# Turning 46 weight blocks early, one by one, through a 1 KB tile into DRAM, and loading them plainly for the last pass

## The chip, the cores and the metric

One core of a Trainium2 chip runs the kernel. The metric is the device time of one execution in microseconds (us). The engines are TensorE (PE; PEld for its weight loads), VectorE (DVE), ScalarE (ACT), GpSimd (POOL) and SyncE (SP), each with its own in-order stream of instructions. All five share 16 DMA engines. Transfers are issued from queues: SyncE's is q1 in the profile, POOL's is q0, ScalarE's is q10.

## The reference

The kernel computes the output of a small network and all gradients of it (12 tensors), for 2048 positions of 576 channels, in bf16.

```python
def _B_ref(x, w1, w3, w2):
    gate = jnp.einsum("bsd,df->bsf", x, w1)
    up = jnp.einsum("bsd,df->bsf", x, w3)
    h = _silu(gate) * up
    return jnp.einsum("bsf,fd->bsd", h, w2)

x = A_u
xn = _layernorm(x, axis=-1)
s = _A_ref(xn, ...)              # a long convolution over the positions, made from A, B, C, log_dt
g = _silu(_B_ref(xn, B_w1, B_w3, B_w2))
out = x + s * g
# returned: out, and the vjp of all of it at grad_out for A_u, the convolution's
# parameters and w1, w3, w2
```

Here w1 and w3 are 576 x 4608 and w2 is 4608 x 576.

## The kernel before

The forward pass (gate and up products, the convolution's kernel, the convolution, the output) takes the first 660 us or so. The function `backward` does the rest.

**Gradient groups.** The 4608 hidden columns are cut into 18 groups of 256 (`NG = 18`). For group `gi`, `phase6_group` makes the gradient at the hidden layer in four steps (stages `h0` to `h3`, matmuls of L1818), which VectorE multiplies onto the tiles `gu_n` and `gg_n` (L1836). These are stored to `GU_dram` and `GG_dram` on SyncE (L1841, stage `stored`). `phase6_grad13` then makes the gradients of w3 and w1 (stages `out_11_0` to `out_11_3`, `out_10_0` to `out_10_3`, matmuls of L1882). `phase6_grad2` makes those of w2 (L1859), one half after `h1`, one after `h3`. ScalarE copies each product out of PSUM (two buffers, `pgw`) into `gw` tiles, and POOL stores them (`grad_store`, L1867).

**What feeds a group.** POOL loads `gg_n` (L1759) and `h_n` (L1744), 1 MB each, two groups ahead into pairs of buffers. ScalarE and VectorE prepare the next group's `gg_n`, `gu_n` and `h_n` from `h3` of the group before on (`phase6_prep`: silu at L1786, its derivative at L1789, products at L1782 and L1783). SyncE turns the block of w2 of a group (`w2T`, L1739) out of rows that it loaded (`w2r`, L1718).

**Beside the groups.** During groups 0 to 5 the backward convolution (`ssm_bwd_conv`) runs on the same engines. Its loads `a` and `gs` and its stores to `gK_dram` go through SyncE. From the end of group 10 on `param_step` reduces the convolution's parameter gradients on VectorE (L1453, L1456), fed by `qT`, `gz` and `pz` through SyncE.

**The last pass.** `phase6_inputs` makes the gradient at the normalized input: for each of 16 blocks of 128 positions, 72 steps of matmuls (L1931) over the 36 column blocks of w1 and of w3. The left operand, `acts`, is `GG_dram` and `GU_dram` turned by SyncE. The right operand is w1 and w3 turned, as blocks of 128 columns by 576: 26 blocks in `wA`, which groups 12 to 16 load, and 46 blocks in eight pieces `wT`. A piece takes the place of a tile that the groups no longer need (`h_n`, `gg_n`, `gu_n`, `w2T`), so it can come only at the end: `load_piece` issues it between group 16 and the beginning of the last pass, with a transfer that turns.

**Order.** Instructions are placed by a scheduler that follows priorities and due times (`at`). `issue_after` puts an instruction behind another in that order. `sp`, `gp` and `sc` chain the instructions of SyncE, POOL and ScalarE in the order in which the code issues them (`sp` only from group 10 on).

The names and lines in the profile are those of this listing:

Of the kernel before, what the change touches and what calls it, by code (L numbers as in the profile page):

```python
# [14 lines left out]
BF16 = mybir.dt.bfloat16  # L15
I32 = mybir.dt.int32
I16 = mybir.dt.int16
P = 128
# [82 lines left out]
class K:  # L101
# [25 lines left out]
    def pool(self, **kw):  # L127
        return self.tc.tile_pool(reuse_waits="tile", **kw)
# [1440 lines left out]
    def backward(self, T0, TG, TQ, TC, TX, gctx, mats):  # L1569
        nc, cfg = self.nc, self.cfg  # L1570
        D, L, LT, F, FT = cfg.D, cfg.L, cfg.LT, cfg.F, cfg.FT
# [6 lines left out]
        pool = self.pool  # L1578
        PS = bass.MemoryType.PSUM
        GP, FE = 11, FT - self.FG // P  # L1580
        with ExitStack() as out:
# [7 lines left out]
            ffn = ExitStack()  # L1589
            elp = out.enter_context(pool(name="e_el", bufs=3))  # L1590
            self.small = out.enter_context(pool(name="e_sm", bufs=1))
            gwp = ffn.enter_context(pool(name="e_gw", bufs=2))
            self.at(T0 - TG)
            self.w2rows = [rowp.tile([P, self.FG // P, cfg.DT * P], BF16, name=f"w2r{i}") for i in range(2)]
            for w2r in self.w2rows:
# [50 lines left out]
            for gi in range(NG):  # L1646
# [9 lines left out]
                for stage in group if gi == 0 else self.phase6_group(gi, cur, elp, gwp, ps_h, ps_gw):  # L1656
                    if stage == "h3" and self.chain and gi + 2 < NG:
                        self.w2Ts[gi + 2] = self.phase6_load_w2(gi + 2, wp)
                    if stage == "h3" or stage[:-1] in ("out_11_", "out_10_") and stage != "out_10_3":
                        next(prep, None)  # L1660
                    if stage in ("h1", "h3"):
                        if gi < NG - 1:
                            w2(gi, stage == "h3")
                        if stage == "h3" and gi + 2 < NG:
                            self.phase6_load_h(gi + 2, T0 + TG * gi, inp)
# [47 lines left out]
    def w2row_load(self, gi):  # L1713
        D = self.cfg.D
        nfl = self.FG // P
        for fl in range(nfl):
            fi = gi * nfl + fl
            self.sp(lambda: self.nc.sync.dma_start(out=self.w2rows[gi % 2][:, fl, 0:D],  # L1718
                                                   in_=self.aps["B_w2"][fi * P:(fi + 1) * P, :]))

    def load_piece(self, wT, pool, tag, ai, f0, n):
        t = pool.tile([P, n, self.cfg.D], BF16, name=f"wT{ai}_{f0}", tag=tag)
        wT.append((ai, f0, n, t))
        self.nat_transpose(t[:], self.aps[("B_w1", "B_w3")[ai]][:, f0 * P:(f0 + n) * P])

    def load_wT_rows(self, part, c):
        ai, f0, n, t = part
# [384 lines left out]
```

## Time and profile before

| | |
|---|---|
| Median of 3 runs | 1701.79 us (1697.92 to 1708.54) |
| The profiled execution's own time | 1704.94 us |
| Its span in the profile | 1703.2 us |
| Mean granted TensorE clock | 0.988 |
| TensorE busy | 1601.0 us, 94% |
| VectorE busy | 1396.6 us, 82% |
| ScalarE busy | 852.8 us, 50% |
| POOL busy | 488.3 us, 29% |
| Time of q1's packets (SyncE) | 64.2% of 16 engines |
| Time of q0's packets (POOL) | 20.5% of 16 engines |
| Time of q10's packets (ScalarE) | 4.0% of 16 engines |

The span runs from the first to the last instruction of the program on the core; the execution's own time holds a little more. Busy time of an engine leaves out the instructions that only issue transfers, wait or branch. All of SyncE is of that kind, so it has no busy time: it is seen through its transfers. A line such as `A L1 <- B L2: 4.6, 3, 1.7` says that A at line 1 waited for B at line 2 for 4.6 us in all, three times, for 1.7 us at most. For a transfer, two durations stand apart: how long its issue held the engine, and "to landing", from the start of the issue until the data had arrived. The landing is known for only some of them.

### The profile page before, as it was taken

The page shows a single profiled execution, that of the slowest core. Times are in us where ns is not written, and L with a number is a line of the kernel's source. Part 1 is how long each engine was busy: PE and PEld are TensorE (multiplying, and loading weights), DVE is VectorE, ACT ScalarE, POOL GpSimd, SP SyncE. Part 2 cuts the span into 40 slices and gives each one's busy share as a digit, 9 for nine tenths or more (in the row PEclk, how much of TensorE's full clock was granted, in tenths as well). Part 3 has the DMA queues.
Part 4 walks back from the last instruction along what each step waited for, and adds up shares of the span by engine and source line. Part 5 has one row for each costly group of instructions (what it writes and reads, how often), then busy time and mean ns, then how long its engine had stood idle before and what let it go on. Part 6 is the DMA issues. An engine that isn't in the chain of part 4 may idle for free. (4 is left out here: it accounts for less than half of the span.)

```text
span 1703.2 us, 34846 instructions
## 1 busy us (share of the span) xinstructions
PE 1601.0 (94%) x13615; PEld 1178.2 (69%) x13615; DVE 1396.6 (82%) x2114; ACT 852.8 (50%) x1536; POOL 488.3 (29%) x786
## 2 busy tenths in 40 slices
PE   6799999999998999999999999999999988999998
PEld 2455555544445777788788788888888866877876
DVE  8779999897974555998996999699999946879765
ACT  6689999866652113756556565555555301000001
POOL 6746676533242111111111111111111252031132
PEclk9899999999999999999999999999999999999999
DMA  7789999989899889766585757799999999999992
GB/s 236 279 307 367 348 366 325 356 284 293 261 274 229 207 197 191 229 197 207 175 218 163 212 181 210 191 259 251 254 217 252 243 243 236 210 200 232 239 205 51
DMA packets 620812, 408.61 MB, mean 240 GB/s; under 512 B 424263, under 2 KB 562007, under 8 KB 616039
## 3 DMA queue, kind: packets, MB, share of 16 engines
q1 hardware_dynamic: 563868, 272.95, 64.2%
q0 software_dynamic: 33984, 114.33, 20.5%
q10 hardware_dynamic: 22794, 19.10, 4.0%
q8 instruction: 107, 1.75, 0.4%
q14 instruction: 59, 0.48, 0.1%
HBM read 128.52 MB, written 189.06 MB: 186 GB/s over the span
## 5 line engine op out<-in xcount | busy, mean ns | idle before, releaser
L1931 PEld LDWEIGHTS <-acts 128*128 128x128 bf16 x2304 | 227.2, 99 | 68.0 <-issue 5.3
L1882 PEld LDWEIGHTS <-xn_bf 128*128 128x128 bf16 x2304 | 224.3, 98 | 35.6 <-issue 9.5
L1453 DVE TENSOR_TENSOR pr_q<-et_ps,pz 128x1024 f32<-128x1024 f32 x144 | 176.1, 1223 | 35.9 <-PE et_ps L1448 27.7
L1867 POOL DMA_DIRECT2D out_dram<-gw x72 | 47.4, 658 | 551.6 <-ACT gw L1884 340.3
L1931 PE MATMUL px<-wT,acts 128*128 128x288 bf16 x1472 | 193.7, 290 | 4.6 <-DMA wT<-in_B_w_dram 4.6
L1456 DVE TENSOR_REDUCE S_all<-pr_q 128x32 f32<-128x1024 f32 x144 | 175.4, 1218 | 3.2
L1074 PEld LDWEIGHTS <-xnT 128*128 128x128 bf16 x1152 | 108.1, 98 | 99.7 <-issue 15.0
L1818 PE MATMUL ph<-w2T,goT 128*128 128x256 bf16 x1440 | 169.1, 273 | 2.3 <-ACT gh L1821 2.3
L1074 PE MATMUL pg<-wmB_w,xnT 128*128 128x512 bf16 x576 | 156.4, 380 | 1.8 <-DVE g_t L1093 1.6
L1074 PE MATMUL pu<-wmB_w,xnT 128*128 128x512 bf16 x576 | 156.8, 379 | 0.0
L1859 PE MATMUL pgw<-go_o,h_n 128*128 128x288 bf16 x1152 | 152.8, 286 | 0.2 <-DVE h_n L1783 0.2
L1818 PEld LDWEIGHTS <-goT 128*128 128x128 bf16 x1440 | 139.2, 98 | 18.8 <-issue 3.0
L1882 PE MATMUL pgw<-gu_n,xn_bf 128*128 128x256 bf16 x1152 | 133.8, 272 | 4.5 <-ACT gw L1863 3.9
L1859 PEld LDWEIGHTS <-h_n 128*128 128x128 bf16 x1152 | 111.8, 98 | 27.6 <-issue 0.8
L1882 PE MATMUL pgw<-gg_n,xn_bf 128*128 128x256 bf16 x1152 | 130.3, 273 | 0.0
L1089 ACT ACTIVATE s_t<-pg 128x512 bf16<-128x512 f32 x144 | 87.4, 607 | 70.5 <-PE pu L1083 51.4
L1821 ACT CAST gh<-ph 128x512 bf16<-128x512 f32 x144 | 80.6, 587 | 79.2 <-PE ph L1818 70.7
L1931 PE MATMUL px<-wA,acts 128*128 128x288 bf16 x832 | 111.7, 291 | 3.5 <-DMA acts<-GU_dram 3.5
L772 POOL COPY KT<-k_s 64x128 bf16<-64x128 bf16 x144 | 95.2, 661 | 66.3 <-ACT k_s L769 61.7
L727 ACT ACTIVATE cs_k<-et_ps 128x512 bf16<-128x512 int16 x216 | 110.3, 627 | 1.1 <-PE et_ps L725 1.0
L1987 ACT ACTIVATE go<-gx 128x576 bf16<-128x576 f32 x16 | 10.9, 683 | 197.8 <-DVE gx L1970 184.2
L1094 ACT CAST u_t<-pu 128x512 bf16<-128x512 f32 x144 | 86.8, 603 | 10.7 <-PE pu L1074 10.5
(308 smaller groups left out, 3120.1 us busy)
## 6 DMA issues: line engine op xcount, KB each, us to landing
U_dram<-u_t POOLq DMA_DIRECT2D x72, 256.0 KB, 4.9
H_dram<-h_t SPq DMA_DIRECT2D x72, 256.0 KB, 5.1
G_dram<-g_t POOLq DMA_DIRECT2D x72, 256.0 KB, 5.1
Q_dram<-q_k SPq DMA_DIRECT2D x36, 512.0 KB, 6.0
gg_n<-G_dram POOLq DMA_DIRECT2D x18, 1024.0 KB, 6.4
h_n<-U_dram POOLq DMA_DIRECT2D x18, 1024.0 KB, 8.1
GG_dram<-gg_n SPq DMA_DIRECT2D x36, 512.0 KB, 7.7
GU_dram<-gu_n SPq DMA_DIRECT2D x36, 512.0 KB, 5.4
```

Source lines behind the costliest of these rows:

```text
L727: self.sin_last = nc.scalar.activation(out=CS[:, :, o:o + 256], in_=pt[:].bitcast(I16)[:, :, 0::2], func=ACT.Sin, scale=6.283184 / 2 ** 16)
L772: nc.gpsimd.tensor_copy(out=KT[64 * hf:64 * hf + 64, :, ch // 9, h, d1:d1 + 8], in_=ks[64 * h:64 * h + 64, :, h, hf].rearrange("p d a -> p ...
L1074: ins = nc.tensor.matmul(pt[:], lhsT=xnT[:, c, ts], rhs=wm[w][:, c, :], start=(q == 0 and c == 0), stop=(q == 1 and c == nfull - 1))
L1089: nc.scalar.activation(out=s_t[:, :, q, :], in_=pgv, func=ACT.Silu)
L1094: self.gate_last = nc.scalar.copy(out=u_t[:, :, q, :], in_=puv)
L1453: nc.vector.tensor_tensor(out=pr[:].rearrange("p r k e -> p r (k e)"), in0=T[x][:].rearrange("p z k h j a -> p (z k h j a)")[:, None].to_b ...
L1456: nc.vector.tensor_reduce(out=self.S_all[:].rearrange("p r (h c) -> p r h c", h=2)[:, :, :, d0:d0 + 2], in_=pr[:].rearrange("p r k (h j a) ...
L1818: self.pe_last = nc.tensor.matmul(ph[j][:, k, :].rearrange("p (a f) -> p a f", f=P), lhsT=lw, rhs=rh, start=(n == 0), stop=(n == nfull))
L1821: self.sc(lambda: nc.scalar.copy(out=gh[:, j], in_=ph[j][:]))
L1859: self.pe_last = nc.tensor.matmul(pgw[pi_][:, 0:pw], lhsT=hn[:, tt, fl * P:(fl + 1) * P], rhs=go_o[:, tt, po:po + pw], start=(tt == 0), st ...
L1882: self.pe_last = nc.tensor.matmul(pw_[:, 0:FG], lhsT=self.xn_bf[:, tt, c * P:(c + 1) * P], rhs=nat[:, tt, :], start=(tt == 0), stop=(tt == ...
L1931: self.pe_last = nc.tensor.matmul(px[pi_][:, 0:pw], lhsT=acts[i][:, ai, fi, :], rhs=w[:, po:po + pw], start=(n == 0), stop=(n == len(steps ...
```

## The change

A tile `w_turn` of 128 x 512 (1 KB in each partition, one buffer) is added. At the stages `h0`, `h2`, `out_11_0`, `out_11_2` and `out_10_0` of groups 0 to 10 one step of the generator `turn_weights` is taken: SyncE turns one block of 512 x 128 of w1 or w3 into the tile, and POOL stores the tile into a DRAM scratch `WT`, laid out as the piece will be read. After the blocks of a piece one more step turns what is left of the 576 rows, 64 of them, for all its blocks at once, so eight pieces make 46 + 8 = 54 steps. `load_piece` then loads a piece plainly from `WT`, at the same place in SyncE's order where it turned it before.

```diff
             gwp = ffn.enter_context(pool(name="e_gw", bufs=2))
+            self.turnp = ffn.enter_context(pool(name="e_turn", bufs=1))
+            self.WT = {}
+            turning = self.turn_weights()
...
+                    if gi < GP and stage in self.TURNS:
+                        next(turning, None)
...
+    PIECES = ((1, 22, 7), (0, 15, 7), (1, 15, 7), (1, 13, 2), (0, 22, 7), (0, 29, 7), (1, 11, 2), (1, 29, 7))
+    TURNS = ("h0", "h2", "out_11_0", "out_11_2", "out_10_0")
+
+    def turn_weights(self):
+        nc, D = self.nc, self.cfg.D
+        nfull = D // P * P
+        store = None
+        for ai, f0, n in self.PIECES:
+            w = self.aps[("B_w1", "B_w3")[ai]]
+            dst = self.WT[ai, f0] = self.dram.tile([P, n, D], BF16, name=f"WT{ai}_{f0}")
+            for f in range(n + 1):
+                t = self.turnp.tile([P, nfull], BF16, name="w_turn")
+                if f < n:
+                    src, out, o = w[0:nfull, (f0 + f) * P:(f0 + f + 1) * P], dst[:, f, 0:nfull], t[:]
+                    i = t[:]
+                else:
+                    rem = D - nfull
+                    o = i = t[:, 0:n * rem].rearrange("p (f d) -> p f d", f=n)
+                    src, out = w[nfull:D, f0 * P:(f0 + n) * P], dst[:, :, nfull:D]
+                with self.tc.issue_after(self.pe_last.ins):
+                    self.nat_transpose(o, src)
+                self.gp(lambda: nc.gpsimd.dma_start(out=out, in_=i))
+                yield
+
     def load_piece(self, wT, pool, tag, ai, f0, n):
         t = pool.tile([P, n, self.cfg.D], BF16, name=f"wT{ai}_{f0}", tag=tag)
         wT.append((ai, f0, n, t))
-        self.nat_transpose(t[:], self.aps[("B_w1", "B_w3")[ai]][:, f0 * P:(f0 + n) * P])
+        self.sp(lambda: self.nc.sync.dma_start(out=t[:], in_=self.WT[ai, f0][:]))
```

## The prediction

> **What bounds the kernel now.** I read the page first, then the stretches, then who waits for whom on each engine, then single tiles.
>
> ```profile
> span 1703.2 us, 34846 instructions
> ...
> PE 1601.0 (94%) x13615; PEld 1178.2 (69%) x13615; DVE 1396.6 (82%) x2114; ACT 852.8 (50%) x1536; POOL 488.3 (29%) x786
> ...
> q1 hardware_dynamic: 563868, 272.95, 64.2%
> ```
>
> TensorE is busy for 94% of the span, so only its gaps can be won; q1, the queue of SyncE with all the turning transfers, is the busiest of the queues. The stretches tell the groups from the last pass (columns: stretch, its length, busy time with count of each engine, granted clock, DMA share, GB/s):
>
> ```profile
> core 0: us, PE busy (x) PEld busy (x) DVE busy (x) ACT busy (x) POOL busy (x), PEclk, DMA share, GB/s
> 690.00:1077.00 387.00, 368.58 (x3648) 317.36 (x3646) 353.81 (x635) 226.46 (x409) 46.86 (x79) 1.00 0.68 198
> 1313.00:1400.00 87.00, 78.25 (x711) 64.65 (x709) 67.31 (x99) 23.14 (x44) 29.15 (x54) 0.96 1.13 241
> 1360.00:1400.00 40.00, 33.66 (x276) 26.42 (x275) 21.40 (x47) 3.14 (x8) 18.47 (x35) 0.91 1.16 243
> 1400.00:1450.00 50.00, 43.29 (x364) 34.17 (x363) 31.18 (x36) 4.93 (x9) 13.74 (x25) 0.97 1.10 241
> ```
>
> Gradient groups 0 to 10 lie in the first: TensorE 95% busy, DMA engines at 0.68, which is room. Around the start of the last pass the DMA engines are full (1.10 to 1.16), TensorE stands still for 6.3 and 6.7 us, and its granted clock dips to 0.91 and 0.97. After it there is nothing to win for a while:
>
> ```profile
> 1450.00:1500.00 50.00, 50.00 (x443) 40.65 (x441) 45.27 (x52) 4.13 (x8) 6.88 (x13) 1.00 1.13 191
> ```
>
> TensorE's waits from 1250 us on (who, for whom, us in total, times, longest):
>
> ```profile
> PE px L1931 <- DMA wT<-in_B_w_dram: 4.6, 3, 1.7
> PE et_ps L1448 <- DVE S_all L1456: 4.1, 1, 4.1
> PE px L1931 <- DMA acts<-GU_dram: 3.5, 1, 3.5
> ```
>
> So 4.6 us are the very pieces that the change reloads, 3.5 us the activations queued behind such pieces on SyncE, 4.1 us are VectorE's. In the groups (640 to 1110 us) no DMA is among TensorE's waits; the largest is
>
> ```profile
> PE et_ps L899 <- DVE ZZ L1385: 8.0, 7, 2.5
> ```
>
> **What the change removes.** Eight turning transfers (the wT pieces, 46 blocks of 576x128) leave the end; eight plain loads of the same 6.8 MB take their places in SyncE's order.
>
> ```profile
> L1739 SPq DMA_TRANSPOSE wT<-in_B_w_dram x8: 1350/4170/9025, 1313.4 to 1393.0; - x8
> ```
>
> A piece held SyncE for 4.2 us in the median. The nearest plain load of that size, beside a turned one (name, KB where told, median us to landing):
>
> ```profile
> gg_n<-G_dram POOLq DMA_DIRECT2D x18, 1024.0 KB, 6.4
> ...
> acts<-GG_dram SPq DMA_TRANSPOSE x17, 8.7
> ```
>
> Both are about 1 MB (a full acts half is 36 blocks of 128x128, 1.18 MB), as is a piece of seven blocks (1.03 MB). 8.7 - 6.4 = 2.3 us less for each of 46 / 7 = 6.6 such pieces is 15 us of DMA time gone from a stretch that is full. That is more than the 4.6 + 3.5 = 8.1 us for which TensorE waited on it, so I take both waits as gone. The clock adds (1 - 0.91) x 40 + (1 - 0.97) x 50 = 5.1 us lost at most to dips after those stops; I take half, 2.5. VectorE's 4.1 us stays. Gain: 8.1 + 2.5 = 10.6 us; its ends are 0 (the queue is as full as before, since qT and acts still turn) and 8.1 + 5.1 = 13.2.
>
> The Trainium skill, Advanced Engine Details and Errata, section X-Bar Transpose (TRN2), says that turning transfers are as fast as plain ones. By it the end would gain nothing; 8.7 against 6.4 us here speaks against it, though the rows differ in queue and hour.
>
> **What it adds.** 54 turns (46 blocks of 512x128, 8 remainders), five a group, on SyncE; 54 stores of up to 128 KB on POOL. There is one tile, so turn k+1 waits for the landing of store k, and store k for the landing of turn k: a single chain of round trips. The ordering hint behind TensorE's last matmul only places a turn in SyncE's order; in the built program a turn waits for the store before it, and for no matmul after the first. But both queues run in order, so the chain is tied to what stands between. On POOL a store stands before nearly every gradient store, and the load of the group after next (gg_n) stands behind store five. On SyncE the stores of GU and GG, the loads of w2T and those of the backward convolution (a, gs) stand behind turns.
>
> A turn by its nearest row, the w2T turns of 128x640 in 690 to 1100 us, and a store by that of gw (144 to 256 KB), same stretch:
>
> ```profile
> L1739 SPq DMA_TRANSPOSE w2T<-w2r x22: 1200/1269/5689, 692.2 to 1099.5; - x22
> ...
> DMA to landing us min/median/max: 2.6/2.6/2.6
> ```
>
> ```profile
> L1867 POOL DMA_DIRECT2D out_dram<-gw x42: 545/568/767, 699.4 to 1099.9; - x42
> ...
> DMA to landing us min/median/max: 2.0/4.0/8.2
> ```
>
> One trip is 2.6 + 4.0 = 6.6 us; five are 33.0. Two of the five queue behind something large. One turn follows the GU and GG stores (2 MB) on q1; what a small transfer there pays is the longest of w2r, which stands behind the same stores:
>
> ```profile
> L1718 SPq DMA_DIRECT2D w2r<-in_B_w_dram x18: 328/454/1382, 697.5 to 1073.0; - x18
> ...
> DMA to landing us min/median/max: 2.1/2.6/8.0
> ```
>
> 8.0 - 2.6 = 5.4 us more. One store follows the 1 MB h_n load on POOL's queue:
>
> ```profile
> L1744 POOL DMA_DIRECT2D h_n<-U_dram x10: 538/539/539, 705.9 to 1063.2; - x10
> ...
> DMA to landing us min/median/max: 5.7/9.4/9.8
> ```
>
> issued 0.5 us after it, it lands no earlier: 9.4 - 0.5 - 4.0 = 4.9 us more. A group's chain: 33.0 + 5.4 + 4.9 = 43.3 us. What a group has comes from the first and last gg_n load, ten groups apart:
>
> ```profile
> L1759 POOL DMA_DIRECT2D gg_n<-G_dram x11: 552/552/554, 691.2 to 1077.0; - x11
> ...
> DMA to landing us min/median/max: 5.0/6.8/11.7
> ```
>
> (1077.0 - 691.2) / 10 = 38.6 us. The chain is 4.7 us a group too long, 47 us over ten groups. What is late next: POOL's gg_n load, then ScalarE's first silu of the next preparation, then (ScalarE runs in order) the copies of pgw, whose two buffers stop TensorE. The cover is read from one group:
>
> ```profile
> 781.17 0.54 POOL L1744 DMA_DIRECT2D h_n<-U_dram  x1
> 786.48 0.76 POOL L1867 DMA_DIRECT2D out_dram<-gw  x1 [4.78 <-ACT gw L1884]
> 793.47 0.76 POOL L1867 DMA_DIRECT2D out_dram<-gw  x1 [6.22 <-ACT gw L1884]
> 794.93 0.55 POOL L1759 DMA_DIRECT2D gg_n<-G_dram  x1 [0.70 <-PE pgw L1893]
> ```
>
> ```profile
> 817.15 1.06 ACT L1786 ACTIVATE gu_n<-gg_n 128x1024 bf16<-128x1024 bf16 x1
> ```
>
> 817.2 - 794.9 - 6.8 = 15.4 us, available once and not per group: a lag that stays is paid no more, one that grows is. Cost in the groups: 47 - 15.4 = 31.6 us. The same rows show where it bites: between h_n and gg_n lie 13.8 us, into which three of the five trips fall.
>
> Ends of this cost. Below: trips at the shortest rows, 2.6 + 2.0 = 4.6 us, five are 23.0, with the two delays 33.3, under 38.6: nothing. A gain here has no source, since nothing is taken out of the groups. Above: the turns of the forward pass with other transfers about,
>
> ```profile
> L1739 SPq DMA_TRANSPOSE hcB<-H_dram x10: 1322/1916/5826, 468.1 to 625.6; - x10
> ...
> DMA to landing us min/median/max: 4.4/6.0/8.9
> ```
>
> at their shortest 4.4, make a trip 8.4 and a group's chain 52.3: (52.3 - 38.6) x 10 - 15.4 = 122 us. Some hcB turns are six times as large, so w2T is nearer; and a stretched group thins the other transfers out and shortens its own trips. I take 6.6.
>
> The remainders' stores write 64 elements a run, in 896 runs; no row shows such a store from POOL. I count them as the others; six large ones at twice the median would add 6 x 4.0 = 24 us to the chain, which the upper end holds. The new load lines, the 54 issues on POOL (0.57 us each of an engine that is 12% busy there) and the 54 on SyncE (1.3 us each, 6 us a group) are hidden as such. In the built order part of the convolution's matmuls and products of groups 4 and 5 change places with the groups' own; their counts are the same, and I count nothing; what it costs if they meet late loads is rival B.
>
> **Sum.** 31.6 - 10.6 = +21.0 us on the span of 1703.2, or on its execution's own 1704.94: 1725.9. That execution is 3.15 above the median of the runs, 1701.79, against which I forecast 1701.8 + 21.0 = 1722.8, say 1723, +1.2%.
>
> **The rivals.** A: the chain fits. It decides at (38.6 - 5.4 - 4.9) / 5 = 5.7 us a trip: below it every turn is hidden in the 32% of DMA time that the groups leave free, the end keeps its gain, and the time is 1701.8 - 10.6 = 1691. For it: the share of 0.68, and gw's shortest landing of 2.0, which a store alone on its queue would have. Against it: the median of 4.0 is that of stores which the chain resembles, and the chain adds traffic. The Trainium skill, DMA: Bandwidth & Descriptors, section Anatomy of one DMA, gives about 2 us as the fixed part of a transfer. An estimate from it, 4 us a trip and 20 a group, is this rival; the median of 4.0 for one store of gw says that here the fixed part is not the whole.
>
> B: the chain is far too long, and the convolution's loads (a, gs), late behind it on SyncE, stop VectorE and through it TensorE's in-order matmuls. At 7.6 us a trip: 48.3 a group, 97 - 15.4 - 10.6 = +71 us, 1773. For it: 8.0 and 9.4 us in the rows above; against it, the self-limit.
>
> C: the groups cost what I say and the end gains nothing, because the stretch stays full of qT and acts: 1701.8 + 31.6 = 1733. For it: share 1.13 after 1450 us, where no piece is turned any more.
>
> **How the numbers follow.** The forecast 0.41, A 0.33, B 0.16, C 0.10. The range 1689 to 1773 holds A's 1691 with its full clock gain of 13.2 and B's 1773; what lies beyond is half of B and little of A. The likeliest case alone, trips of 6.2 to 7.0 us, runs from 1703 to 1743. About 1% (17 us) is what a measurement of this kernel can tell from no change. Faster by more than that needs more than the whole of A's gain, 13.2 us: 0.04, taken from A. Within 1%: the rest of A (0.29), the lower third of the forecast (0.14) and 0.01 of C: 0.44. Slower: 0.27 of the forecast, B, and 0.09 of C: 0.52.
>
> **What would show it.** In the changed profile the gg_n loads of groups 0 to 10 stand 42 to 43 us apart instead of 38.6, POOL waits for turns landing (w_turn) ahead of its stores, SyncE for stores (WT) landing ahead of turns, and TensorE's busy share there falls from 95% to about 88%. At the end TensorE's waits for wT and acts are gone and the clock stays near 1. Wrong I am if gg_n loads keep their 38.6 us (A), if they stand over 46 us apart or VectorE waits for a or gs (B), or if TensorE still waits for weights or activations at 1360 to 1405 us plus the shift (C).

## The result, and the profile after

The changed kernel takes 1770.24 us in the median of 6 runs, the kernel before 1704.22 us on the same chip: a ratio of 1.0388 (95% interval 1.0343 to 1.0434), 66 us slower. The forecast was 21 us slower; 1770 lies just inside its range, 1689 to 1773. The profiled execution took 1774.58 us. Lines after the new function lie 29 lower than before: L1788 is the gg_n load (before L1759), L1773 the h_n load, L1768 every turning transfer, L1815 the first silu, L1811 and L1812 VectorE's products, L1847 and L1850 the hidden layer's matmuls and ScalarE's copies of them, L1870 the stores of GU and GG, L1892 ScalarE's copy of a w2 product, L1911 the matmuls of the w1 and w3 gradients, L1896 the gradient stores, L1960 the last pass. L1747 is the new store, L1753 the new plain load.

The page of the changed kernel:

```profile
span 1772.8 us, 34974 instructions
...
PE 1611.2 (91%) x13555; PEld 1186.9 (67%) x13615; DVE 1399.7 (79%) x2114; ACT 852.7 (48%) x1536; POOL 517.5 (29%) x840
...
q1 hardware_dynamic: 566492, 279.74, 65.1%
```

TensorE's work is the same, and its share is down from 94% to 91%. It is busy some 10 us longer, at a mean granted clock of 0.971 instead of 0.988; the rest of the added time went into gaps. The single tiles tell where. First the kernel before, then the changed one (count, ns min/median/max, first to last start):

```profile
L1931 PE MATMUL px<-wA,acts x832: 286/286/448, 1365.6 to 1689.2; 128*128 128x288 bf16 x167
L1759 POOL DMA_DIRECT2D gg_n<-G_dram x18: 534/552/554, 655.2 to 1294.5; - x18
```

```profile
L1960 PE MATMUL px<-wA,acts x832: 286/286/444, 1428.6 to 1758.7; 128*128 128x288 bf16 x167
L1788 POOL DMA_DIRECT2D gg_n<-G_dram x18: 534/547/732, 654.0 to 1357.7; - x18
...
L1788 POOL DMA_DIRECT2D gg_n<-G_dram x11: 539/539/732, 689.3 to 1137.8; - x11
```

The last pass begins at 1428.6 instead of 1365.6 us, 63.0 later, and from there to the end lie 1772.8 - 1428.6 = 344.2 us instead of 337.6, 6.6 more. The span is 69.6 longer. So the groups cost twice the 31.6 us forecast, and this profile shows no gain at the end. The eleven gg_n loads, which stood 38.6 us apart, stand (1137.8 - 689.3) / 10 = 44.9 us apart; 43.3 was forecast.

The stretches (length, busy time with counts, granted clock, DMA share, GB/s): the groups, 40 us near the start of the last pass, and the whole last pass.

```profile
690.00:1137.80 447.80, 398.46 (x3807) 339.93 (x3805) 373.64 (x669) 233.10 (x420) 74.98 (x128) 0.95 0.76 200
...
1436.00:1476.00 40.00, 35.80 (x275) 27.54 (x273) 12.40 (x28) 2.89 (x6) 19.28 (x38) 0.91 1.10 253
1428.60:1772.80 344.20, 309.10 (x2603) 246.72 (x2601) 236.84 (x325) 32.07 (x63) 88.68 (x163) 0.96 1.02 197
```

TensorE is busy for 398.5 / 447.8 = 89% of the groups (95% before). Who waits for whom there (us in total, times, longest; POOL and SyncE from 690 to 1151 us, then TensorE and ScalarE from 640 to 1180, and last TensorE before the change, from 640 to 1110):

```profile
POOL WT L1747 <- DMA w_turn<-in_B_w_dram: 359.1, 49, 21.0
...
SPq L1768 <- DMA WT<-w_turn: 117.4, 43, 5.9
SPq L1768 <- DMA w_turn<-in_B_w_dram: 83.3, 32, 6.4
```

```profile
PE pgw L1911 <- ACT gw L1892: 25.0, 9, 9.2
...
ACT gu_n L1815 <- DMA gg_n<-G_dram: 23.6, 6, 9.7
```

```profile
PE pgw L1882 <- ACT gw L1863: 2.6, 10, 0.3
```

This is the path that the prediction named, link by link: POOL stands for turns, SyncE for the store and the turn before, ScalarE's silu for gg_n (before, it never did), TensorE for ScalarE's copies (and 15.1 us for those of L1850, 2.3 before). The new tile's own rows give the trip:

```profile
L1747 POOL DMA_DIRECT2D WT<-w_turn x51: 539/545/939, 689.9 to 1146.5; - x51
...
DMA to landing us min/median/max: 1.9/2.5/6.5
...
L1768 SPq DMA_TRANSPOSE w_turn<-in_B_w_dram x51: 1123/1164/6345, 696.4 to 1148.6; - x51
...
DMA to landing us min/median/max: 2.6/3.2/8.5
```

Fifty trips took 1146.5 - 689.9 = 456.6 us, 9.1 each and 45.7 for five. The stores' landings and the starts of the issues divide the mean trip: 3.1 us until the store has landed, 0.9 until SyncE issues the next turn, 5.1 from there to the next store, for which POOL waits until the turn has landed (the landings of seven turns alone are known). The shortest trips take 4.9 to 5.4 us. Two things make the others longer.

The first is a 1 MB load in flight. Sixteen turns were issued within 4 us behind POOL's load of gg_n or h_n, and the stores of 14 of them start 0.9 to 1.4 us after that load has landed. From such a turn to its store pass 7.6 us in the mean behind gg_n and 6.9 behind h_n; the median of the other 35 is 3.3. One of them (start, us held, engine; POOL's rows, then SyncE's):

```profile
1087.30 0.54 POOL L1788 DMA_DIRECT2D gg_n<-G_dram  x1
...
1095.59 0.68 POOL L1747 DMA_DIRECT2D WT<-w_turn  x1 [6.68 <-DMA w_turn<-in_B_w_dram]
...
1088.03 1.19 SPq L1768 DMA_TRANSPOSE w_turn<-in_B_w_dram  x1
```

The load and the turn both take 7.0 us to landing, so the turn, a remainder of 32 KB on the other queue, lands 0.7 us after the 1 MB.

The second is that SyncE issues a turn late. It does so in eight of the fifty trips, by 45 us in all; in the others the turn goes as soon as the store has landed. The longest such delay up to group 5:

```profile
871.82 0.54 POOL L1747 DMA_DIRECT2D WT<-w_turn  x1 [7.52 <-DMA w_turn<-in_B_w_dram]
872.36 0.54 POOL L1896 DMA_DIRECT2D out_dram<-gw  x1
872.89 0.54 POOL L1773 DMA_DIRECT2D h_n<-U_dram  x1
893.50 0.55 POOL L1747 DMA_DIRECT2D WT<-w_turn  x1 [20.07 <-DMA w_turn<-in_B_w_dram]
```

```profile
870.63 7.17 SPq L1404 DMA_DIRECT2D gK_dram<-gk_st  x4
877.85 5.86 SPq L1870 DMA_DIRECT2D GU_dram<-gu_n  x2
883.80 3.12 SPq L1870 DMA_DIRECT2D GG_dram<-gg_n  x2
887.03 3.24 SPq L1768 DMA_TRANSPOSE w_turn<-in_B_w_dram  x1
```

POOL's store of 871.8 has landed 6.3 us later and lets the next turn go, but that turn stands in SyncE's order behind the stores of gK, GU and GG, which hold SyncE for 7.2 + 5.9 + 3.1 = 16.2 us. Of these, 5.9 are put down to VectorE by SyncE's waits from 868 to 888 us:

```profile
SPq L1870 <- DVE h_n L1812: 5.0, 1, 5.0
SPq L1870 <- DVE gg_n L1811: 0.9, 1, 0.9
```

The turn is issued at 887.0, 8.9 us late; POOL has stood since 873.4, and this trip took 893.5 - 871.8 = 21.7 us.

At the start of the last pass (1428.6 to 1525.5 us) TensorE waits thus:

```profile
PE et_ps L1448 <- DMA gz<-gK_dram: 6.1, 1, 6.1
PE et_ps L1448 <- DVE pr_q L1453: 4.9, 2, 4.4
PE px L1960 <- DMA wT<-WT: 4.2, 1, 4.2
```

The wait for activations (3.5) is gone and that for pieces is nearly what it was (4.6, now 4.2). The parameter steps' waits for gz and VectorE have grown, from 0.9 and 4.1 us.

### The profile page after: what moved, and what is told of

Read it like the earlier page. It is cut to its first block, busy times and chain, and to the rows that moved or that the text cites. A ratio compares the mean times of both kernels' runs of the same rounds, so it can differ in the third digit from the quotient of the medians.

```text
span 1772.8 us, 34974 instructions
## 1 busy us (share of the span) xinstructions
PE 1611.2 (91%) x13555; PEld 1186.9 (67%) x13615; DVE 1399.7 (79%) x2114; ACT 852.7 (48%) x1536; POOL 517.5 (29%) x840
## 5 line engine op out<-in xcount | busy, mean ns | idle before, releaser
L1911 PEld LDWEIGHTS <-xn_bf 128*128 128x128 bf16 x2304 | 227.5, 99 | 70.3 <-issue 41.0
L1960 PEld LDWEIGHTS <-acts 128*128 128x128 bf16 x2304 | 227.3, 99 | 63.6 <-issue 4.6
L1960 PE MATMUL px<-wT,acts 128*128 128x288 bf16 x1472 | 195.4, 291 | 4.2 <-DMA wT<-WT 4.2
L1847 PE MATMUL ph<-w2T,goT 128*128 128x256 bf16 x1440 | 174.5, 278 | 15.1 <-ACT gh L1850 15.1
L1911 PE MATMUL pgw<-gu_n,xn_bf 128*128 128x256 bf16 x1152 | 139.6, 280 | 36.4 <-ACT gw L1892 35.8
L1847 PEld LDWEIGHTS <-goT 128*128 128x128 bf16 x1440 | 141.8, 100 | 34.3 <-issue 16.1
L1074 PE MATMUL pg<-wmB_w,xnT 128*128 128x512 bf16 x548 | 151.7, 381 | 4.6 <-DVE g_t L1093 2.6
L1074 PE MATMUL pu<-wmB_w,xnT 128*128 128x512 bf16 x551 | 152.1, 380 | 1.0
L1747 POOL DMA_DIRECT2D WT<-w_turn x54 | 32.0, 593 | 396.3 <-DMA w_turn<-in_B_w_dram 390.3
L1911 PE MATMUL pgw<-gg_n,xn_bf 128*128 128x256 bf16 x1152 | 131.2, 274 | 0.0
L1850 ACT CAST gh<-ph 128x512 bf16<-128x512 f32 x144 | 80.8, 588 | 97.9 <-PE ph L1847 72.9
L1960 PE MATMUL px<-wA,acts 128*128 128x288 bf16 x832 | 109.7, 288 | 0.0
L1896 POOL DMA_DIRECT2D out_dram<-gw x72 | 48.1, 671 | 193.3 <-ACT gw L1913 139.3
```

What stands on the lines that cost most here:

```text
L1074: ins = nc.tensor.matmul(pt[:], lhsT=xnT[:, c, ts], rhs=wm[w][:, c, :], start=(q == 0 and c == 0), stop=(q == 1 and c == nfull - 1))
L1847: self.pe_last = nc.tensor.matmul(ph[j][:, k, :].rearrange("p (a f) -> p a f", f=P), lhsT=lw, rhs=rh, start=(n == 0), stop=(n == nfull))
L1850: self.sc(lambda: nc.scalar.copy(out=gh[:, j], in_=ph[j][:]))
L1896: self.gp(lambda: self.nc.gpsimd.dma_start(out=out, in_=in_))
L1911: self.pe_last = nc.tensor.matmul(pw_[:, 0:FG], lhsT=self.xn_bf[:, tt, c * P:(c + 1) * P], rhs=nat[:, tt, :], start=(tt == 0), stop=(tt == ...
L1960: self.pe_last = nc.tensor.matmul(px[pi_][:, 0:pw], lhsT=acts[i][:, ai, fi, :], rhs=w[:, po:po + pw], start=(n == 0), stop=(n == len(steps ...
```

## The experiments

Each run is compared with the kernel before on its chip. Two columns come from its own profile. "Groups" is the time from the first gg_n load to the first px matmul, less the 1365.6 - 655.2 = 710.4 us of before; "last pass" is from the first px matmul to the end of the span. For the changed kernel: 1428.6 - 654.0 - 710.4 = +64.2, and 344.2.

| run | what | ratio (95%) | groups | last pass |
|---|---|---|---|---|
| before | | 1 | 0 | 337.6 |
| changed | | 1.0388 (1.0343 to 1.0434) | +64.2 | 344.2 |
| e1 | plain pieces alone | 0.9965 (0.9919 to 1.0010) | +9.2 | 330.6 |
| e12 | e1 again, for its ratio | 0.9980 (0.9945 to 1.0016) | | |
| e2 | groups alone | 1.0392 (1.0315 to 1.0469) | +65.8 | 352.0 |
| e3 | two tiles | 1.0099 (1.0049 to 1.0148) | +21.5 | 331.9 |
| e4 | two tiles, late store | 1.0067 (1.0029 to 1.0105) | +22.4 | 328.6 |
| e5 | late store on SyncE | 1.0431 (1.0325 to 1.0537) | +43.7 | 333.0 |
| e6 | uncoupled | 1.0356 (1.0284 to 1.0428) | +34.3 | 328.8 |
| e9 | uncoupled, tied | 1.0084 (1.0042 to 1.0125) | +13.7 | 338.3 |
| e10 | store on SyncE, tied | 1.0030 (0.9987 to 1.0074) | +20.9 | 328.6 |
| e7 | three a group, 27 steps | 1.0049 (1.0007 to 1.0090) | +0.3 | 348.0 |
| e13 | four a group, 43 steps | 1.0092 (1.0038 to 1.0145) | +25.5 | 334.0 |
| e11 | three a group, 54 steps | 1.0433 (1.0370 to 1.0496) | +44.2 | 358.4 |
| e8 | plain loads for turns | 1.0275 (1.0192 to 1.0358) | +43.1 | 339.6 |
| e14 | all behind GU, GG | 1.0535 (1.0462 to 1.0609) | +97.2 | 333.8 |
| e15 | early places | 1.0466 (1.0407 to 1.0525) | +75.7 | 334.9 |
| e16 | early, two tiles | 1.0064 (1.0027 to 1.0101) | +8.1 | 337.0 |
| e17 | as e16, seven pieces | 1.0021 (0.9982 to 1.0060) | +10.4 | 341.7 |

How far one profile can be read: e1 changes nothing in the groups and still shows +9.2 there, most of it one stop of 7.4 us (its waits from 1077 to 1400 us),

```profile
PE pgw L1908 <- ACT gw L1889: 8.7, 6, 7.4
```

and the last pass runs from 328.8 to 352.0 us where pieces are turned (before, e2, e6, e8, e9; mean 339.3) and from 328.6 to 344.2 where they are loaded plainly (changed, e1, e3, e4, e5, e10, e14, e15, e16; mean 333.6; e11, whose turning runs into it, is left out). So a group cost under about 10 us and any price of the end are not read from one profile. e16 and e17 show the same: TensorE, VectorE, ScalarE and POOL run the same instructions in the same order up to group 8, and yet by the first silu of group 6, counted from that of group 0, e17 is 9.0 us later than the kernel before, and e16 is at its place to 0.1 us.

**The end by itself (e1, e12).**

```diff
...
-                    if gi < GP and stage in self.TURNS:
-                        next(turning, None)
...
-        self.sp(lambda: self.nc.sync.dma_start(out=t[:], in_=self.WT[ai, f0][:]))
+        src = self.G_dram[f0 % 16].rearrange("p l f -> p (l f)")[:, 0:n * self.cfg.D]
+        src = src.rearrange("p (n d) -> p n d", n=n)
+        self.sp(lambda: self.nc.sync.dma_start(out=t[:], in_=src))
```

> The end alone: no block is turned in the groups, and the eight pieces are loaded plainly at the end, with the same sizes and the same 8 KB runs, from the forward pass's scratch G_dram. The turning of these 46 blocks is left out, so the pieces hold other numbers than the weights. The prediction's step (the end gains 10.6 us: 8.1 of waits and 2.5 of clock) expects 1704.2 - 10.6 = 1694. Its rival C (the stretch stays full of qT and acts) expects 1704. The trace after the change, read as it stands (last pass 344.2 us instead of 337.6), would put plain loads at +6.6: 1711.

> The end alone once more, with more rounds: no turning in the groups, pieces loaded plainly from G_dram, so that they hold other numbers than the weights. The first time gave 0.9965 (0.9919 to 1.0010). The prediction's step of 10.6 us is 0.9938, its lower end is 1.0, the last pass of the first profile (330.6 against 337.6 us, 7.0 less) is 0.9959.

The mean of the two ratios is 0.9973, and its half-width sqrt(0.0046^2 + 0.0036^2) / 2 = 0.0029: a gain of 4.7 us, give or take 4.9, and the two means of the last pass above are 5.7 us apart the same way. The loss of 6.6 us read off the changed profile is not confirmed; the 10.6 forecast lies just outside. TensorE's waits in e1's whole last pass (1371.7 to 1702 us) begin with:

```profile
PE et_ps L1448 <- DVE pr_q L1453: 7.9, 3, 6.5
PE et_ps L1448 <- DMA gz<-gK_dram: 4.7, 1, 4.7
PE px L1957 <- DMA wT<-G_dram: 3.2, 2, 1.7
```

With 1.1 us more for VectorE they are 16.9 us; before, from 1365.6 us on, they were 19.8: 4.6 for pieces, 3.5 for activations, 3.5 for gz and 8.2 for VectorE. The activations' wait went and that for pieces shrank by 1.4, but 2.0 came back at gz and VectorE. The granted clock in the first 40 and the next 50 us of the last pass is 1.00 and 0.86 in e1, and 0.91 and 0.97 before: no gain there.

**The groups by themselves (e2).**

```diff
-        self.sp(lambda: self.nc.sync.dma_start(out=t[:], in_=self.WT[ai, f0][:]))
+        self.nat_transpose(t[:], self.aps[("B_w1", "B_w3")[ai]][:, f0 * P:(f0 + n) * P])
```

> The groups alone: the 54 turns and stores stay, and the pieces are turned at the end as before, so the stored blocks are read by nobody. If the whole cost lies in the groups (the last pass began 63.0 us later) and the end gains or loses nothing, 1704.2 + 63.0 = 1767. If the plain loads do gain 10.6 us, which the late groups hide, 1770.2 + 10.6 = 1781. If they cost 6.6 us, 1764.

It costs 1.0392, as much as the whole change. The cost lies in the groups; the end's few us do not show beside an interval of 13 either way.

**A second tile (e3), and stores issued a step later (e4).**

```diff
...
-            self.turnp = ffn.enter_context(pool(name="e_turn", bufs=1))
+            self.turnp = ffn.enter_context(pool(name="e_turn", bufs=2))
```

> Two w_turn tiles instead of one (the space is taken from a second buffer of gev), else as changed. Theory 1, the single chain of trips: a trip took 9.0 us in the mean (5.1 from a turn's issue to its store's issue, 3.0 to the store's landing, 0.9 of SyncE's delay); with two tiles two trips overlap, 4.5 us each and 22.5 a group, below the 38.6 that a group has, so the gg_n loads stand 38 to 39 us apart again and the time is 1695 to 1711. Theory 2, POOL's order: a store holds POOL until its turn has landed (359 us of waits in 690 to 1151 us), whatever the number of tiles, so at most the store's landing is saved, 3.0 x 54 = 160 us of chain, but the standing behind SyncE stays: 1725 to 1750. Theory 3, traffic: the 54 turns and stores slow everything, in any arrangement: 1760 to 1775.

```diff
...
-                self.gp(lambda: nc.gpsimd.dma_start(out=out, in_=i))
+                if store is not None:
+                    self.gp(store)
+                store = lambda out=out, i=i: nc.gpsimd.dma_start(out=out, in_=i)
                 yield
+        self.gp(store)
```

> Two tiles, and the store of turn k is issued one step later, in the place of store k+1, so that POOL finds its turn landed. Theory 1 (chain) and theory 2 (POOL's order) both expect the groups' cost gone: gg_n loads 38 to 39 us apart, POOL's wait for w_turn under 40 us, time 1704 give or take what the end does (1694 to 1711). Theory 3 (traffic) expects 1760 to 1775. What tells theories 1 and 2 apart is this run against the one with two tiles alone: the same time by theory 1, 20 to 45 us less by theory 2.

POOL's waits, two tiles first, then late stores:

```profile
POOL WT L1747 <- DMA w_turn<-in_B_w_dram: 177.1, 21, 23.9
```

```profile
POOL WT L1749 <- DMA w_turn<-in_B_w_dram: 149.2, 19, 23.2
```

The second tile takes two thirds of the cost away (64.2 to 21.5). Storing later adds nothing that shows (the two intervals overlap), so theory 2 falls. In both POOL still stands 23 us for the longest turn. All runs with two tiles, and e6, also take gev's second buffer away; that was not tried by itself.

**Stores moved or uncoupled, with and without a tie (e5, e6, e9, e10).** e5 is e4 with `nc.sync.dma_start` ahead of the next turn. e6:

```diff
+        still = self.turnp.tile([P, nfull], BF16, name="w_still")
+        nc.gpsimd.memset(still[:], 0.0)
...
-                    i = t[:]
+                    i = still[:]
...
```

> Two tiles, and the store of turn k is issued on SyncE, just ahead of turn k+1, instead of on POOL. POOL then holds no store of a turned block. Late stores on POOL still left the last pass beginning 22.9 us later than before, with waits of POOL for turns of 16.9 us in group 5 and 23.2 us in group 11, each followed by a stop of TensorE (5.0 and 7.0 us). If POOL standing for late turns is that rest, it is gone here: the last pass begins within 5 us of before, its length is 328 to 332 us, and the time is 0.995 of before (1693 to 1704 against 1702). If the rest is the added traffic, or SyncE's own lateness, it stays: 1.005 to 1.012 (1710 to 1722).

> All 54 turns and all 54 stores, each at its place and on its queue, but the stores read a tile of zeros that nothing writes any more, so no store waits for a turn and no turn for a store; the pieces are turned at the end as before. The turned blocks are written nowhere and nobody reads them. If the cost is the coupling (chain and standing), the gg_n loads keep 38.6 to 39.7 us and the time is 1.000 of before (1697 to 1709 against 1702). If a part of it is the traffic or the issues, that part is seen here alone: 1.012 (1722) if the rest of 20 us that late stores left is traffic, 1.039 (1768) if all is.

Both miss, for a reason that neither theory had. e6's turns up to 752 us,

```profile
L1770 SPq DMA_TRANSPOSE w_turn<-in_B_w_dram x43: 1122/1135/2033, 553.5 to 744.8; - x43
```

and its stores:

```profile
L1749 POOL DMA_DIRECT2D WT<-w_still x54: 539/545/988, 752.6 to 1163.2; - x54
```

43 of 54 turns ran before the groups, among the forward pass's transfers on SyncE; in e5 it was 39 up to 750 us. The first gg_n load is 28.8 us late in e6 and 23.5 in e5, and between the first two loads lie 32.1 and 35.8 us more than before, most of what the table puts down to their groups. What had kept a turn at its place was the wait for the store before it. From the second gg_n load on (752.1 us) e6 lost 1428.7 - 752.1 - (1365.6 - 691.2) = 2.2 us: 54 stores on POOL that wait for nothing, with 11 turns, cost no more than that. With a word written by POOL that each turn waits for, the turns keep their places (in e10 the same line in e5):

```diff
...
+                self.gp(lambda: nc.gpsimd.memset(t[0:1, 0:2], 0.0))
                 with self.tc.issue_after(self.pe_last.ins):
                     self.nat_transpose(o, src)
...
```

> As the uncoupled kernel, whose turns ran far ahead of their places (some 35 of them before the groups, where they held up the forward pass by 61 us), but with every turn tied to its place: POOL writes one word of the tile at the step, and the turn waits for that. Two tiles, so that a turn waits for no other turn; the stores read rows of xn_bf, so no store waits for a turn and no turn for a store; the pieces are turned at the end as before, and nobody reads the blocks. If the coupling is the whole cost, the 54 turns and 54 stores at their places are free: TensorE's groups keep their distance, the last pass begins within 4 us of before, 0.998 to 1.003 (1698 to 1707 against 1702). If traffic and queue places carry the 20 us that two tiles left, 1.010 to 1.014 (1719 to 1726).

> The whole change in another form: two tiles, every turn tied to its place by a word that POOL writes, and the store of turn k on SyncE just ahead of turn k+1, so POOL holds no store of a turned block; the pieces are loaded plainly. Theory of the coupling: the groups cost 0 to 4 us and the end gains 6: 0.996 to 0.999 of before (1695 to 1700 against 1702). If the stores on SyncE make its own work late (w2T, a, gs, GU and GG behind them), the cost is that of late stores on POOL: 1.005 to 1.010.

e9 was not free: 14 us by its ratio and its profile. POOL still waits 85.8 us there, before its word, for the turn before the last, so it is not wholly uncoupled, and the 14 us bound what traffic costs from above. e10 lies between its two theories; as a whole it cannot be told from the kernel before, and the +20.9 of its one profile is of an execution of 1724 us, 8 above its median.

**How many a group (e7, e13, e11).**

```diff
-    TURNS = ("h0", "h2", "out_11_0", "out_11_2", "out_10_0")
+    TURNS = ("h0", "out_11_0", "out_10_0")
...
+        for ai, f0, n in self.PIECES[0:4]:
...
```

> Three steps a group (h0, out_11_0, out_10_0) instead of five, with one tile and stores on POOL as changed; only the first four pieces (23 blocks, 27 steps, groups 0 to 8) are turned early, the other four at the end as before. Theory of the chain: it has a threshold; three trips of 9.0 us are 27 us of the 38.6 that a group has, so the groups cost 0 to 8 us and, with half of the end's gain, the time is 0.998 to 1.003 of before (1698 to 1707 against 1702). Theory of the standing: every store costs its share, 63 x 27 / 54 = 32 us less 3: 1.017 (1731).

> Four steps a group (h0, h2, out_11_0, out_10_0) with one tile and stores on POOL as changed; the first six pieces (37 blocks, 43 steps, groups 0 to 10) are turned early, the other two at the end as before. A trip took 9.0 us in the mean with five a group. If the cost has the threshold of the chain, four trips are 36 us of 38.6 to 39.7 and the groups cost what their unevenness leaves, 0 to 12 us: 1.000 to 1.008 of before (1702 to 1716 against 1702). If it grows with the steps, 63 x 43 / 54 = 50 us: 1.027 to 1.031.

Three cost nothing in the groups (+0.3), four 25.5 (16 by the ratio), five 64.2: there is a threshold, but between three and four, below the 4.3 that 38.6 / 9.0 gives. With four the trips themselves are longer:

```profile
L1747 POOL DMA_DIRECT2D WT<-w_turn x43: 540/547/919, 698.1 to 1145.3; - x43
```

(1145.3 - 698.1) / 42 = 10.6 us a trip, 42.6 for four. A trip has no fixed price: here SyncE issues the next turn 2.0 us late in the mean, not 0.9, and a store lands in 3.5 us, not 3.1. e7 as a whole is not faster (+8 us). In its last pass of 348.0 us TensorE waits 21.6 us for gz and VectorE, where it was 11.7 before; why was not found out.

> All 54 steps, one tile, stores on POOL as changed, but three a group over groups 0 to 17 instead of five over 0 to 10. Theory of the chain with a threshold: three trips are 27 us of the 36 to 39 that a group has, so groups 0 to 10 cost under 3 us as they did with 27 steps; from group 11 on SyncE's transfers are chained with the parameter steps, trips may be longer (up to 12 us before 36 are reached), so the later groups cost 0 to 10 us: 0.997 to 1.004 of before (1697 to 1709 against 1702). Theory of a cost per step: 63 us for 54 steps, as with five a group: 1.033 to 1.039.

A miss: three a group are not free from group 11 on. Its gg_n loads in these groups:

```profile
L1788 POOL DMA_DIRECT2D gg_n<-G_dram x7: 539/539/559, 1099.1 to 1358.2; - x7
```

(1358.2 - 1099.1) / 6 = 43.2 us apart, 14.4 a trip, where before they were (1294.5 - 1077.0) / 6 = 36.3. There the turns share SyncE with the parameter steps' loads, and SyncE issues a turn 5.9 us late in the mean, against 0.9 before group 11. The turning runs on into the last pass (its last turn at 1443.6 us, the first px matmul at 1425.1), which is 20.9 us longer.

**Plain loads in place of turns (e8).**

```diff
-                    self.nat_transpose(o, src)
+                    nc.sync.dma_start(out=t[:].rearrange("p (c q) -> p c q", q=P),
+                                      in_=w[0:nfull, (f0 + f % n) * P:(f0 + f % n + 1) * P].rearrange("(c p) q -> p c q", p=P))
...
```

> Plain loads of 512 x 128 in place of the 54 turns, into the same single tile, with the same stores behind them; the pieces are turned at the end as before, and what the stores write is read by nobody. From a turn's issue to its store's issue lay 5.1 us in the mean. If the turning makes them long, a plain load lands like w2r (3.8 us in the median after the change), a trip is 1.3 us shorter, five are 6.5, of the 7.2 us by which a group is over: 1.002 to 1.010 of before (1705 to 1719 against 1702). If they are long because of what stands about them on the queue and in the DMA engines, whatever the kind, nothing changes: 1.035 to 1.042 (1762 to 1773).

```profile
L1746 SPq DMA_DIRECT2D w_turn<-in_B_w_dram x53: 367/383/5941, 696.9 to 1150.7; - x53
...
DMA to landing us min/median/max: 2.3/3.1/8.2
```

In between. By the seven landings known of each, a plain load lands hardly sooner than a turn of the changed kernel (2.6, 3.2 and 8.5 us), but it holds SyncE for 0.4 us instead of 1.2. A trip is (1141.8 - 690.3) / 52 = 8.7 us instead of e2's (1150.4 - 694.3) / 50 = 9.1, and the groups cost 43.1 us instead of 65.8. By these two profiles a third of the cost is the price of turning against loading; two thirds stay with plain loads. Here too loads that follow gg_n or h_n wait for the 1 MB: 7.2 us to their store in the mean, against a median of 3.2 for the others.

**Where in the group (e14, e15).**

```diff
-    TURNS = ("h0", "h2", "out_11_0", "out_11_2", "out_10_0")
+    TURNS = ("out_11_0", "out_11_1", "out_11_2", "out_11_3", "out_10_0")
```

> All 54 steps, five a group, one tile, stores on POOL as changed, but taken at out_11_0, out_11_1, out_11_2, out_11_3 and out_10_0, all behind the stores of GU and GG in the order of the code, none at h0 or h2 ahead of them. In the changed kernel the longest trips (14.6 to 22.6 us, eight of 50) are those whose turn SyncE issued 3 to 10 us late, behind those stores; without them the period would be 45.8 - 45.2 / 10 = 41.3 us against 39.7, and the groups cost 15 to 25 us: 1.007 to 1.013 of before (1714 to 1724 against 1702). If the place on SyncE does not matter, because the next trip waits for the next thing, the cost stays near 63 us: 1.034 to 1.041.

> All 54 steps, one tile, stores on POOL as changed, but taken at h0, h1, h2, h3 and out_11_0: four of five stores stand ahead of POOL's h_n load and one between it and the gg_n load. With all five between them the period was 47.7 us and the groups cost 97 us; with three (the changed kernel) 45.8 and 63. If it is the number of trips between h_n and gg_n that counts (17 us more for each of the two trips added), one trip there costs 63 - 2 x 17 = 29 us or less: 1.000 to 1.020 of before (1702 to 1736 against 1702). If the chain's length alone counts (five trips of 9.0 us in 38.6 to 39.7), the place is all one: 1.033 to 1.041 (1758 to 1772).

Out of the way of GU and GG the change is worse, not better (+97), and with one trip between h_n and gg_n it is no cheaper either (+75.7). So neither the wait behind GU and GG nor the number of trips between the two loads sets the cost; with one tile and five a group every order costs 64 us or more. Why e14 costs 20 to 30 us more than the other two stays open.

**Early places and two tiles (e16, e17).** e16 has `("h0", "h1", "h2", "h3", "out_11_0")` and two tiles; e17 the same with `self.PIECES[0:7]`.

> The same early places with two tiles. Two tiles alone gave 1.0099 of before, places in the middle. By the number of trips between h_n and gg_n, this is the cheapest form of the change: groups 0 to 10 us, the end gains 4: 0.998 to 1.004. By the chain's length alone it is as two tiles were: 1.008 to 1.012.

> Two tiles, early places (h0, h1, h2, h3, out_11_0), and only the first seven pieces (39 blocks, 46 steps): turning ends in group 9, ahead of the parameter steps; the eighth piece is turned at the end as before. With all 54 steps TensorE's groups 1 to 11 kept their distance to 0.2 us, and the one stop (8.2 us between groups 11 and 12) was a parameter step's wait for gz and qT, behind the last turns on SyncE. If that is so, the groups cost under 2 us here; the time is that, less what plain loads gain at the end (4.4 us in the mean of the two runs of the end alone, 3.9 for seven of eight): 0.997 to 1.001 of before (1697 to 1704 against 1702). If the steps cost otherwise than by their chain, 1.005 to 1.010.

e16's groups in one stretch, the same window as the prediction's first:

```profile
690.00:1077.00 387.00, 368.38 (x3655) 317.37 (x3653) 354.40 (x639) 224.67 (x406) 75.66 (x128) 1.00 0.87 227
```

TensorE is busy for 368.38 us where it was 368.58 before, at a clock of 1.00, with the DMA engines at 0.87 instead of 0.68 and 48 turns and 50 stores inside. In this execution their traffic costs nothing up to group 11. It is one of the three fastest of twelve, and e17's, with the same steps up to group 8, is not like it in the same window:

```profile
690.00:1077.00 387.00, 363.86 (x3543) 311.87 (x3541) 345.95 (x623) 220.22 (x405) 71.47 (x120) 0.98 0.83 221
```

So with two tiles and early places most of the cost is gone, and by the ratios 11 us (e16) and 4 us (e17, within its interval) are left. e16's profile has one stop to show for it, which came later (1077 to 1400 us; e16, then e17):

```profile
PE et_ps L1448 <- DMA gz<-gK_dram: 5.3, 1, 5.3
PE et_ps L1530 <- DVE ST L1516: 2.8, 1, 2.8
```

```profile
PE pgw L1914 <- ACT gw L1895: 1.6, 6, 0.3
PE et_ps L1448 <- DVE pr_q L1453: 1.4, 1, 1.4
```

With the turning ended in group 9 the wait for gz is gone, as expected, but e17 is not faster than before (1.0021, from 0.9982 to 1.0060); 9.0 of its +10.4 us arise up to group 6, and what holds it there stays open. No version run here beats the kernel before by more than its interval.

## Why the prediction was right and wrong

The direction and the mechanism were right: one tile makes a chain of trips, the chain is longer than a group, gg_n comes late, and TensorE pays through ScalarE. The size was wrong by a factor of three, 21 against 66 us, and that 1770 lies in the range is owed to rival B's 1773 at its end, not to the forecast's sum. These steps failed.

**The slack (15.4 us): read at the wrong place.** It was taken at one load in the middle, at 794.9. What counts is the cover where the chain ends, at group 12. The load and the silu there, before and after:

```profile
1116.42 0.55 POOL L1759 DMA_DIRECT2D gg_n<-G_dram  x1 [2.47 <-DVE S_all L1456]
...
1129.54 1.06 ACT L1786 ACTIVATE gu_n<-gg_n 128x1024 bf16<-128x1024 bf16 x1
```

```profile
1183.35 0.73 POOL L1788 DMA_DIRECT2D gg_n<-G_dram  x1
...
1191.24 1.06 ACT L1815 ACTIVATE gu_n<-gg_n 128x1024 bf16<-128x1024 bf16 x1 [9.46 <-DMA gg_n<-G_dram]
```

Before, 13.1 us lay between them; after, 7.9, of which gg_n's landing is nearly all. So 5.2 us of cover were there, not 15.4: 10.2 us. (The landing of 6.8 us in it is a median over gg_n's loads and some stores of GG; the loads alone land in 5.9.)

**The lag (47 us): the largest term of the error.** The interval grew to 44.9 instead of 43.3 us: over the same ten, 448.5 - 385.8 = 62.7 us of lag, 15.7 more than forecast. And 54 steps at five a group are eleven groups, not ten: the next load stood 45.6 us on (39.4 before), 6.2 more. With the load of group 1 already 1.9 us earlier than before, 31.6 + 10.2 + 15.7 + 6.2 - 1.9 = 61.8, which is the silu's delay (1191.2 - 1129.5 = 61.7); the last pass is late by 63.0. With 4.7 us gained at the end 57 us are accounted for; the other 9 lie within the intervals and stay open.

**The trip (6.6 us, and 10.3 for two delays): right in sum, wrong in its parts.** Five trips were forecast at 43.3 us and took 45.7. The turns took 5 x 5.1 = 25.5 us, not 13.0; the 2.6 taken for one was the only landing known of the 22 w2T turns in its row. The stores took 5 x 3.1 = 15.5, not 20.0 and 4.9 more. SyncE's lateness was 5 x 0.9 = 4.5, against the 5.4 for GU and GG. The errors cancelled, which is luck. The 4.9 us for the store behind h_n never came: with the chain late, every such store started 6.9 us or more after the load was issued, when h_n had landed. What paid for the 1 MB loads was the turn, behind h_n and also behind gg_n, and the delay behind gg_n, 7.6 - 3.3 = 4.3 us a group, was put at nothing without a reason. (Stores that do go 0.5 us after h_n, in e6, land 0.2 to 1.3 us after it, so the rule that the term went by holds.) The shortest trips, 4.9 us, lie under rival A's 5.7, so by undisturbed transfers A would have been chosen, wrongly. The Trainium skill's 2 us of fixed part (DMA: Bandwidth & Descriptors, Anatomy of one DMA, for transfers that GpSimd issues) lies near the shortest store here, 1.9 us, and says nothing of such delays.

**The end (10.6 us; ends 0 and 13.2).** Mis-sized: 4.7 us, give or take 4.9. The step that failed took both waits, 8.1 us, as gone. In e1 the wait for acts (3.5) went, that for wT fell only from 4.6 to 3.2, and 2.0 came back in waits for gz and VectorE, which were not priced: 2.9 us in all. The clock's 2.5 did not come (1.00 and 0.86 in e1, 0.91 and 0.97 before).

**The traffic, costed at nothing:** borne out by e16's profile up to group 11 and by e6's, not by e17's; up to some 10 us of it are not excluded. **The remainders' stores** were counted as the others, with 24 us in the upper end: in the changed profile the six large ones land in 2.8 to 6.4 us, 4.1 in the mean, against 3.0 for the block stores, so they put some 7 us on the chain.

**The rivals.** B's 1773 is nearest to the 1770 measured, but hardly by its path: VectorE's waits for a were 7.5 us in 640 to 1150 us (none before), and TensorE's for ZZ 13.6 us, against 8.0. Its 48.3 us a group were too many, its slack too large and its groups one too few, which cancelled. C's observation (TensorE still waits for pieces) holds, its zero is within the interval. A's free groups were seen only with fewer turns a group (e7) or with a second tile and early places (e16's profile).

## What to carry to other kernels

Work that is split into small steps through one buffer is a chain: price each trip with the large transfers that are in flight beside it, on whichever queue, and with what stands ahead of its issue, not by its own transfers alone; then compare it with the period of the loop that carries it; past that, every round adds its excess. A second buffer took away two thirds of the cost, and together with early places most of it. Read the cover of a late load where the lag ends, at its smallest, not in one group in the middle. And a gain at the end of a kernel that is smaller than the scatter of that stretch needs a run of its own.

## What the runs showed of the hardware

Turned against plain loads of the same 512 x 128 block, in the chain: landing 2.6, 3.2 and 8.5 us (shortest, median, longest of seven) against 2.3, 3.1 and 8.2, issue 1.2 against 0.4 us. The Trainium skill (Advanced Engine Details and Errata, X-Bar Transpose (TRN2)) calls them as fast as plain ones; by landing the runs nearly agree, but in a chain the difference came to a third of the cost (e8 against e2, one profile each). A small turn issued on SyncE's queue within 4 us behind a 1 MB load on POOL's was followed by its store 0.9 to 1.4 us after the load had landed in 14 of 16 cases; with plain loads (e8) it was within 1.4 us in 13 of 16. Raising the DMA share from 0.68 to 0.87 left TensorE's busy time in the same window unchanged in e16 (368.58 and 368.38 us); in e17, at 0.83, it was 363.86. The granted clock, 1.00 there before, was 0.95 in the changed kernel's groups, with the stops, and 1.00 in e16's, without them.
